# Merged prefix scans with resetting columns, turn counting on ScalarE and permuted reads in a two-expert kernel

## The chip, the cores and the metric

The kernel runs on one core of a Trainium2 chip. The metric is device time in microseconds (us) of one execution. The core has TensorE (PE in the profile, its weight loads PEld), VectorE (DVE), ScalarE (ACT), GpSimd (POOL) and SyncE (SP), which here only issues DMAs.

## The reference

A gated linear attention with a complex decay, followed by two dense expert layers:

```python
# attention: q, k, v, a_re, a_im are [4, 8, 768, 48] float32
mag = np.sqrt(a_re * a_re + a_im * a_im)
scale = np.minimum(mag, 0.999) / (mag + 1e-06)
a_re_n, a_im_n = (a_re * scale, a_im * scale)
for t in range(S):
    ar, ai = (a_re_n[:, :, t, :, None], a_im_n[:, :, t, :, None])
    new_re = ar * S_re - ai * S_im
    new_im = ar * S_im + ai * S_re
    kv = np.einsum('bhd,bhe->bhde', k[:, :, t], v[:, :, t])
    S_re, S_im = (new_re + kv, new_im)
    y[:, :, t] = np.einsum('bhd,bhde->bhe', q[:, :, t], S_re)
# x = y as [3072, 384]
x = (sigmoid(x @ w_gate) * (x @ w_val)) @ w_out      # first expert, d_ff 1536
h = x @ w_in
out = (h * sigmoid(h)) @ w2_out                      # second expert, d_ff 2048
```

The expert weights are float64 in memory; x is float32.

## The kernel before

**Attention in chunks.** The 3072 tokens are cut into 24 chunks of 128 time steps (`C = 128`), six for each batch element (`CPB = 6`); a chunk holds all 8 heads, so it has 384 columns (48 features times 8 heads). Each step's decay is taken apart into a magnitude m and a phase. Within a chunk the recurrence becomes matrix products, for which every key is scaled by the product of the magnitudes behind it (suffix product r), every query by the product up to it over the whole chunk's product (p), and both are turned by the summed phase f.

**Stages of a chunk.** Each is a function `s_...`, and a table of "beats" (`sched`, `starts`) says in which beat a chunk's stage is emitted, so that several chunks are under way at once. `s_nat1`, `s_nat2`, `s_nat2b` (L428 to L473) compute magnitude and tangent with time on the partitions; L472 writes the magnitudes m. `s_nat3` (L478) takes the arctangent on ACT. `s_perm` (L425) copies k and q on ACT. L472, L478 and L425 change the order of the columns from head-major to feature-major: they read in the order of memory and write with a stride of 8 elements (`perm`, L415). `s_den1` (L486 to L514) transposes m and the phases on PE into two PSUM tiles (`tr4`, L480: time now runs along the columns, 3 blocks of 128 partitions), and DVE scans each of the 3 blocks: three reversed scans for r (L500), three for p (L506), three for f (L510), each over 127 or 128 columns. Between them it multiplies out the chunk's whole product `pe` (L502, L503) and inverts it (L504). The phase sum is brought into one turn by three DVE instructions over 384 columns (L511 to L513: scale and add a large constant, subtract it and scale, subtract from f), and its last column is kept for the next chunk (`ca`, L514). `s_den2` takes sines on ACT (L520 to L522). `s_den3` (L524) transposes k and q, multiplies, copies the chunk's product behind the scaled keys (L533, L534), and 12 DMAs on SP regroup the result by head (`kst`, `qst`, L546). `s_mix1` to `s_mix3` are the products on PE (`ps_k` L559, `ps_a` L565, `ps_s`, `ps_y`), masked on DVE (L566).

**PSUM.** The attention's PSUM tiles (`ps_t`, `ps_k`, `ps_a`, `ps_s`, `ps_y`) share one pool of 3 buffers (`patt`, L374). The two tiles that `s_den1` scans are two of these three until the scans have read them.

**Experts.** A float64 weight tile is loaded by SP, turned into a float32 with rounding by ACT, DVE and POOL (`w_decode`, L338 to L341), and split into two parts (`w_split`, L347 on ACT, L348 on DVE or POOL in turn). Every product is three matmuls of such parts (`mm3`, L363 to L365). The first expert runs over nine blocks of 2 or 3 chunks, 12 steps of f each; in a step the gate's product `ps_g`, its tanh (L820, ACT), the value's product `ps_v`, their product `sg` (L823, DVE, which frees `ps_v`), the two parts `hh` (L829, ACT) and `hl` (L831, DVE), and the product back into `acc`. Between the halves of the steps the beats of later chunks are emitted. The second expert (L853 to L907) begins when attention is over; its weight tiles take the SBUF that attention leaves.

**Order.** PE's instructions run in the order in which the program emits them. The order on DVE, ACT, POOL and SP is set by a planner, which lists instructions by a simulated time line. Each engine then works through its list in order: an instruction that waits holds up all behind it.

Of the kernel before, what the change touches and what calls it, by code (L numbers as in the profile page):

```python
# [9 lines left out]
F32 = mybir.dt.float32  # L10
F32R = mybir.dt.float32r
I32 = mybir.dt.int32
U32 = mybir.dt.uint32
AF = mybir.ActivationFunctionType
ALU = mybir.AluOpType
# [230 lines left out]
def tile_kernel(ctx, tc, q, k, v, a_re, a_im, w_gate, w_val, w_out, w2_in, w2_out, out):  # L246
# [6 lines left out]
    F2 = w2_in.shape[1] // 256  # L253
    KD = DM // 128
    C = 128
    NCH = NT // C
    CPB = S // C
    R2 = 2 * D
# [116 lines left out]

    vz = stk.tile([128, H, EA], F32, tag="vz", name="vz")
    sdz = stk.tile([R2, H, EA], F32, tag="sdz", name="sdz")
    for t in (vz, sdz):
        G.memset(t, 0.0)
    ch = [dict() for _ in range(NCH)]  # L380
    RAMP = CFG["ramp"]

# [30 lines left out]
            ch[c][nm] = x  # L413

    def perm(t):  # L415
        return t.rearrange("p (d h) -> p h d", h=H)

    def heads(t):
        return t.rearrange("p (h d) -> p h d", h=H)

    def s_perm(c):
        z = ch[c]
        for nm in ("k", "q"):
            t = new(c, nat, [128, DM], nm + "p")
            A.copy(perm(t), z[nm])  # L425
            z[nm + "p"] = t

    def s_nat1(c):  # L428
# [48 lines left out]
        need(ATAN if c >= RAMP else TRIG)  # L477
        lut(A.activation(perm(z["X"][:, 0]), heads(z["Y"][:, 0]), AF.Arctan, scale=-1.0))  # L478

    def tr4(src):  # L480
        ps = patt.tile([128, KD, C], F32, tag="att", name="ps_t")
        for j in range(KD):
            PE.transpose(ps[:, j, :], src[:, j * 128:(j + 1) * 128], ident)
        return ps

    def s_den1(c):  # L486
        z = ch[c]
        mT = tr4(z["m"])
        pT = tr4(z["X"][:, 0])
        p_ = new(c, den, [128, KD, C], "p")  # L490
        rx = new(c, den, [128, KD, C + 1], "r")
        r_ = rx[:, :, 0:C]
        f_ = new(c, den, [128, KD, C], "f")
        n_ = new(c, den, [128, KD, C], "n")
        pe_ = den.tile([128, 2, KD], F32, tag="pe", name="pe", bufs=2)
        ca_ = den.tile([128, KD], F32, tag="ca", name="ca", bufs=2)
        z.update(p=p_, rx=rx, f=f_, n=n_, pe=pe_, ca=ca_)
        V.memset(r_[:, :, C - 1:C], 1.0)
        for j in range(KD):
            V.tensor_tensor_scan(  # L500
                r_[:, j, 0:C - 1][:, ::-1], mT[:, j, 1:C][:, ::-1], mask[:, 0:C - 1], 1.0, ALU.mult, ALU.bypass)
        V.tensor_tensor(pe_[:, 0], r_[:, :, 0], mT[:, :, 0], ALU.mult)  # L502
        V.tensor_scalar(pe_[:, 0], pe_[:, 0], TINY, None, ALU.max)  # L503
        V.reciprocal(pe_[:, 1], pe_[:, 0])  # L504
        for j in range(KD):
            V.tensor_tensor_scan(  # L506
                p_[:, j, :], mT[:, j, :], mask, pe_[:, 1, j:j + 1], ALU.mult, ALU.bypass)
        for j in range(KD):
            init = 0.0 if c % CPB == 0 else ch[c - 1]["ca"][:, j:j + 1]
            V.tensor_tensor_scan(f_[:, j, :], pT[:, j, :], mask, init, ALU.add, ALU.bypass)  # L510
        V.tensor_scalar(n_, f_, INV_2PI, MAGIC, ALU.mult, ALU.add)  # L511
        V.tensor_scalar(n_, n_, MAGIC, TWO_PI, ALU.subtract, ALU.mult)
        V.tensor_tensor(f_, f_, n_, ALU.subtract)  # L513
        V.tensor_copy(ca_, f_[:, :, C - 1])  # L514

    def s_den2(c):
        z = ch[c]
        n_, f_ = z["n"], z["f"]
        need(SIN if c >= RAMP else TRIG)
        lut(A.activation(n_, f_, AF.Sin, scale=UNIT))  # L520
        lut(A.activation(f_, f_, AF.Sin, scale=UNIT / 2))
        A.activation(f_, f_, AF.Square, scale=math.sqrt(2.0))  # L522

    def s_den3(c):  # L524
        z = ch[c]
        n_, f_, p_, rx = z["n"], z["f"], z["p"], z["rx"]
        r_ = rx[:, :, 0:C]
        kT = tr4(z["kp"])
        qT = tr4(z["qp"])
        kc = new(c, den, [128, KD, C + 1], "kc")  # L530
        V.tensor_tensor(r_, r_, kT, ALU.mult)
        V.tensor_tensor(p_, p_, qT, ALU.mult)
        V.tensor_copy(kc[:, :, C], z["pe"][:, 0])  # L533
        V.tensor_copy(rx[:, :, C], z["pe"][:, 0])  # L534
        V.scalar_tensor_tensor(kc[:, :, 0:C], f_, 1.0, r_, ALU.subtract, ALU.mult)
        G.tensor_tensor(r_, n_, r_, ALU.mult)
        V.scalar_tensor_tensor(f_, f_, 1.0, p_, ALU.subtract, ALU.mult)
        G.tensor_tensor(n_, n_, p_, ALU.mult)
        if c < RAMP and c % 2:
            kst = xp.tile([128, H, C + 1], F32, tag="xl", name="kst")[:R2]  # L540
        else:
            kst = stk.tile([R2, H, C + 1], F32, tag="kst", name="kst")
        qst = stk.tile([R2, H, C], F32, tag="qst", name="qst", bufs=2)
        for t, dst, off in ((kc, kst, 0), (rx, kst, D), (f_, qst, 0), (n_, qst, D)):
            for j in range(KD):
                SP.dma_start(dst[off + j * DI:off + (j + 1) * DI], t[:, j, :])  # L546
        z.update(kst=kst, qst=qst)

    def s_mix1(c):
        z = ch[c]  # L550
        kst, qst = z["kst"], z["qst"]
        kn = new(c, stk, [128, H, R2], "kn")
        am = stk.tile([128, H, C], F32, tag="am", name="am")
        hh = H // 2

        def turn(g):
            ps = patt.tile([128, hh, R2], F32, tag="att", name="ps_k")
            for h in range(hh):
                PE.transpose(ps[:, h, :], kst[:, g * hh + h, 0:C], ident[:R2, :R2])  # L559
            A.copy(kn[:, g * hh:(g + 1) * hh], ps)  # L560

        def score(g):
            ps = patt.tile([128, hh, C], F32, tag="att", name="ps_a")
            for h in range(hh):
                PE.matmul(ps[:, h, :], kst[:, g * hh + h, 0:C], qst[:, g * hh + h, :], start=True, stop=True)  # L565
# [52 lines left out]
    def s_mix2a(c):  # L618
        z = ch[c]
        A.copy(spread(vz), tails(z["v"]))  # L620
        if c % CPB:
            sd = st2.tile([R2, H, D], F32, tag="sd", name="sd", bufs=1)
            V.tensor_tensor(
                sd, ch[c - 1]["st"], z["kst"][:, :, C:C + 1].to_broadcast([R2, H, D]), ALU.mult)
            z["sd"] = sd
            V.tensor_copy(spread(sdz), tails(sd))

# [48 lines left out]
    def beats_for(i):  # L676
        return pos(bstart[i] + blocks[i] - 1, "mix3") + 1

# [1 line left out]
    w1 = {}  # L680
    raws, decs = {}, {}
    order1 = [(f, j) for f in range(F1) for j in range(3)]
# [73 lines left out]
    with tc.manual_schedule(engines={getattr(mybir.EngineType, e) for e in CFG["man"]}):  # L756
# [92 lines left out]
        moe_out(*prev)  # L849
        finish1(*fin)  # L850

# [102 lines left out]
```

## Time and profile before

| | us |
|---|---|
| median of 3 runs | 1206.17 (1203.48 to 1208.49) |
| span of the profiled execution | 1202.7 |
| PE busy in it | 1073.7 (89%) |
| DVE busy | 795.2 (66%) |
| ACT busy | 636.0 (53%) |
| POOL busy | 265.3 (22%) |

The span runs from the first to the last instruction of one execution; a run's time has what lies around it too. Shares of the whole span mix stages with different limits, so the rows below are by stage. Busy times of one engine can overlap by some tens of ns from one instruction to the next: a mean duration is longer than busy time over count.

### The profile page before, as it was taken

Reading aid. Unit: us, or ns where it says so; the run is one execution under the profiler, and the core shown is the slowest. Engines: PE = TensorE matmul, PEld = TensorE weight load, DVE = VectorE, ACT = ScalarE, POOL = GpSimd, SP = SyncE. Lnnn points to the kernel's source line nnn. Section 1 sums busy time; section 2 is a strip of 40 time slices with the busy share of each in tenths; the row PEclk is TensorE's granted clock in tenths of the full one; section 3 lists DMA queues with packets and bytes.
Section 4 is the critical chain, followed back from the end, with each engine's and each line's share of the span. In section 5 each row is a group of like instructions: output and inputs, shape, how many; then the busy total and the mean of one; then the engine's idle time right before and its main releaser. Section 6 shows DMA issues by size and latency. Waiting matters only on the chain. (4 is left out here: it accounts for less than half of the span.)

```text
span 1202.7 us, 21016 instructions
## 1 busy us (share of the span) xinstructions
PE 1073.7 (89%) x7814; PEld 1043.9 (87%) x7814; DVE 795.2 (66%) x1625; ACT 636.0 (53%) x1213; POOL 265.3 (22%) x258
## 2 busy tenths in 40 slices
PE   0376689999999999999999987899999999999997
PEld 0266579998999999999999987789999999999997
DVE  7899988688767866768667389977643434434343
ACT  5566677556666555566564255577533333333332
POOL 6555643222222222222221056500000000000000
PEclk9988799999999999999999999999999999999999
DMA  9256533343322333433221236599310101000000
GB/s 239 80 148 167 137 85 76 63 108 80 74 60 61 94 71 68 95 71 80 61 47 54 67 135 214 174 368 372 136 33 8 40 2 40 25 15 20 1 21 23
DMA packets 216765, 111.63 MB, mean 93 GB/s; under 512 B 132304, under 2 KB 209488, under 8 KB 216656
## 3 DMA queue, kind: packets, MB, share of 16 engines
q1 hardware_dynamic: 216656, 110.21, 33.8%
q8 instruction: 64, 1.05, 0.4%
q14 instruction: 45, 0.37, 0.1%
HBM read 81.79 MB, written 9.44 MB: 76 GB/s over the span
## 5 line engine op out<-in xcount | busy, mean ns | idle before, releaser
L887 DVE SCALAR_TENSOR_TENSOR sg<-sg,ps_h 128x384 f32<-128x384 f32 x128 | 70.8, 553 | 143.0 <-ACT sg L885 142.9
L885 ACT ACTIVATE sg<-ps_h 128x384 f32<-128x384 f32 x128 | 63.0, 492 | 167.7 <-PE ps_h L365 167.7
L365 PE MATMUL acc<-w,hl 128*128 128x384 f32 x384 | 129.2, 336 | 0.4
L363 PE MATMUL acc<-w,hh 128*128 128x384 f32 x384 | 128.6, 335 | 0.6 <-ACT hh L891 0.6
L363 PE MATMUL ps_v<-xh,w 128*128 128x384 f32 (+1 forms) x324 | 112.0, 346 | 19.2 <-DVE sg L823 19.1
L364 PE MATMUL acc<-w,hh 128*128 128x384 f32 x384 | 128.3, 334 | 0.0
L363 PE MATMUL ps_h<-xh,w 128*128 128x384 f32 x384 | 128.3, 334 | 0.0
L365 PE MATMUL ps_h<-xh,w 128*128 128x384 f32 x384 | 128.3, 334 | 0.0
L364 PE MATMUL ps_h<-xl,w 128*128 128x384 f32 x384 | 128.3, 334 | 0.0
L364 PE MATMUL acc<-hl,w 128*128 128x384 f32 (+1 forms) x324 | 106.7, 329 | 14.6 <-DVE hl L831 14.6
L893 DVE TENSOR_TENSOR hl<-sg,hh 128x384 fp32r<-128x384 f32 x128 | 71.3, 557 | 63.0 <-ACT hh L891 62.9
L363 PE MATMUL ps_g<-xh,w 128*128 128x384 f32 (+1 forms) x324 | 109.2, 337 | 3.7 <-ACT sg L820 3.1
L829 ACT CAST hh<-sg 128x384 fp32r<-128x384 f32 (+1 forms) x108 | 51.2, 474 | 108.7 <-DVE sg L823 108.6
L364 PE MATMUL ps_g<-xl,w 128*128 128x384 f32 (+1 forms) x324 | 105.4, 325 | 3.1 <-DVE xl L645 3.1
L364 PE MATMUL ps_v<-xl,w 128*128 128x384 f32 (+1 forms) x324 | 106.2, 328 | 0.0
L365 PE MATMUL ps_v<-xh,w 128*128 128x384 f32 (+1 forms) x324 | 106.2, 328 | 0.0
L363 PE MATMUL acc<-hh,w 128*128 128x384 f32 (+1 forms) x324 | 104.9, 324 | 0.6 <-ACT hh L829 0.6
L365 PE MATMUL ps_g<-xh,w 128*128 128x384 f32 (+1 forms) x324 | 105.2, 325 | 0.0
L365 PE MATMUL acc<-hh,w 128*128 128x384 f32 (+1 forms) x324 | 104.5, 323 | 0.0
L823 DVE SCALAR_TENSOR_TENSOR sg<-sg,ps_v 128x384 f32<-128x384 f32 (+1 forms) x108 | 54.4, 504 | 69.0 <-PE ps_v L365 69.0
L891 ACT CAST hh<-sg 128x384 fp32r<-128x384 f32 x128 | 65.6, 513 | 61.9 <-DVE sg L887 61.1
L341 POOL TENSOR_TENSOR raw<-raw,rnd 128x384 int32<-128x384 int32 x68 | 78.5, 1157 | 85.3 <-ACT rnd L338 33.2
(134 smaller groups left out, 2937.3 us busy)
## 6 DMA issues: line engine op xcount, KB each, us to landing
raw<-in_moe_w_out_dram SPq DMA_DIRECT2D x56, 384.0 KB, 6.6
raw<-in_moe_w_in_dram SPq DMA_DIRECT2D x32, 384.0 KB, 8.0
raw<-in_moe_w_gate_dram SPq DMA_DIRECT2D x24, 384.0 KB, 6.0
raw<-in_moe_w_val_dram SPq DMA_DIRECT2D x24, 384.0 KB, 6.4
kst<-kc SPq DMA_DIRECT2D x72, 64.5 KB, 2.7
kst<-r SPq DMA_DIRECT2D x72, 64.5 KB, 2.9
ri<-in_a_re_dram SPq DMA_DIRECT2D x24, 192.0 KB, 3.8
ri<-in_a_im_dram SPq DMA_DIRECT2D x24, 192.0 KB, 3.9
```

What stands on the lines that cost most here:

```text
L341: G.tensor_tensor(hi, hi, rnd, ALU.add)
L363: PE.matmul(o, lhi, rhi, start=first, stop=False)
L364: PE.matmul(o, lhi, rlo, start=False, stop=False)
L365: PE.matmul(o, llo, rhi, start=False, stop=last)
L823: V.scalar_tensor_tensor(sg[:, :n], sg[:, :n], 1.0, psv[:, :n], ALU.add, ALU.mult)
L829: A.copy(hh[:, :n], sg[:, :n])
L885: lut(A.activation(sg[:, :BT2], ps[:, :BT2], AF.Tanh, scale=0.5))
L887: V.scalar_tensor_tensor(sg[:, :BT2], sg[:, :BT2], 1.0, ps[:, :BT2], ALU.add, ALU.mult)
L891: A.copy(hh[:, :BT2], sg[:, :BT2])
L893: V.tensor_tensor(hl[:, :BT2], sg[:, :BT2], hh[:, :BT2].bitcast(F32), ALU.subtract)
```

## The change

- **Scans.** The transposed tiles get a 129th column in each of the 3 blocks (`CX = C + 1`), and one scan runs over all 387 columns (386 for p and f). In the extra column the magnitude is 0, so the running product is reset, and an added tensor restarts it: `edge` (1 in these columns) for r, `starts_` (the inverse of the chunk's product) for p. For f the multiplier `inner` is 0 there, and the phase tile holds the carried phase. So r now includes its own step, its first column is the chunk's product, and what reads r is shifted by a column. `edge`, `inner` and `starts_` are filled once, on POOL.
- **Around the scans.** DVE fills the extra columns of both PSUM tiles (a memset, and a copy or memset) and inverts 3 columns; L498, L502, L503 and the two copies L533, L534 go. One copy of the chunk's product into `kc` is made by ACT.
- **Turns.** ACT multiplies f by 1/(2 pi) and writes an int32; DVE subtracts that many turns in one instruction.
- **Permutation.** L472, L478 and L425 write contiguously and read with a stride of 48 elements (L472 from two inputs).

```diff
     def perm(t):
-        return t.rearrange("p (d h) -> p h d", h=H)
+        return t.rearrange("p (d h) -> p d h", h=H)
     def heads(t):
-        return t.rearrange("p (h d) -> p h d", h=H)
+        return t.rearrange("p (h d) -> p d h", h=H)
...
-            A.copy(perm(t), z[nm])
+            A.copy(perm(t), z[nm].rearrange("p h d -> p d h"))
...
-        V.memset(r_[:, :, C - 1:C], 1.0)
-        for j in range(KD):
-            V.tensor_tensor_scan(
-                r_[:, j, 0:C - 1][:, ::-1], mT[:, j, 1:C][:, ::-1], mask[:, 0:C - 1], 1.0, ALU.mult, ALU.bypass)
-        V.tensor_tensor(pe_[:, 0], r_[:, :, 0], mT[:, :, 0], ALU.mult)
-        V.tensor_scalar(pe_[:, 0], pe_[:, 0], TINY, None, ALU.max)
-        V.reciprocal(pe_[:, 1], pe_[:, 0])
-        for j in range(KD):
-            V.tensor_tensor_scan(
-                p_[:, j, :], mT[:, j, :], mask, pe_[:, 1, j:j + 1], ALU.mult, ALU.bypass)
-        for j in range(KD):
-            init = 0.0 if c % CPB == 0 else ch[c - 1]["ca"][:, j:j + 1]
-            V.tensor_tensor_scan(f_[:, j, :], pT[:, j, :], mask, init, ALU.add, ALU.bypass)
-        V.tensor_scalar(n_, f_, INV_2PI, MAGIC, ALU.mult, ALU.add)
-        V.tensor_scalar(n_, n_, MAGIC, TWO_PI, ALU.subtract, ALU.mult)
-        V.tensor_tensor(f_, f_, n_, ALU.subtract)
+        V.memset(mT[:, :, C:CX], 0.0)
+        if first:
+            V.memset(pT[:, 0:KD - 1, C:CX], 0.0)
+        else:
+            V.tensor_copy(pT[:, 0:KD - 1, C], ch[c - 1]["ca"][:, 1:KD])
+        V.tensor_tensor_scan(flat(rx)[:, ::-1], flat(mT)[:, ::-1], edge[:, ::-1], 0.0, ALU.mult, ALU.add)
+        V.reciprocal(starts_[:, 0:KD * CX:CX], rx[:, :, 0])
+        N = KD * CX - 1
+        V.tensor_tensor_scan(flat(p_)[:, :N], flat(mT)[:, :N], starts_[:, 1:], starts_[:, 0:1], ALU.mult, ALU.add)
+        V.tensor_tensor_scan(
+            flat(f_)[:, :N], inner[:, :N], flat(pT)[:, :N], 0.0 if first else ch[c - 1]["ca"][:, 0:1], ALU.mult, ALU.add)
+        f_ = f_[:, :, 0:C]
+        A.activation(n_.bitcast(I32), f_, AF.Copy, scale=INV_2PI)
+        V.scalar_tensor_tensor(f_, n_.bitcast(I32), -TWO_PI, f_, ALU.mult, ALU.add)
         V.tensor_copy(ca_, f_[:, :, C - 1])
...
-        V.tensor_copy(kc[:, :, C], z["pe"][:, 0])
-        V.tensor_copy(rx[:, :, C], z["pe"][:, 0])
-        V.scalar_tensor_tensor(kc[:, :, 0:C], f_, 1.0, r_, ALU.subtract, ALU.mult)
+        A.copy(kc[:, :, 0], rx[:, :, 0])
+        V.scalar_tensor_tensor(kc[:, :, 1:CX], f_, 1.0, r_, ALU.subtract, ALU.mult)
```

## Rows read from the trace of the kernel before

**Rows 1.** Stretches: length, busy PE, PEld, DVE, ACT, POOL; PE clock; DMA
```profile
28.00:172.00 144.00, 88.95 (x718) 81.23 (x719) 134.22 (x266) 89.47 (x167) 82.64 (x75) 0.88 0.50 129
...
60.00:180.00 120.00, 84.53 (x730) 78.91 (x730) 111.77 (x221) 78.26 (x147) 68.05 (x60) 0.86 0.51 135
180.00:360.00 180.00, 168.98 (x1615) 164.39 (x1613) 135.18 (x322) 113.28 (x197) 42.41 (x42) 0.97 0.36 77
360.00:690.00 330.00, 319.89 (x2670) 311.10 (x2669) 225.34 (x518) 184.25 (x303) 67.60 (x67) 1.00 0.30 69
690.00:800.00 110.00, 92.97 (x490) 87.70 (x489) 97.77 (x146) 63.52 (x148) 53.62 (x48) 0.95 0.62 207
```

**Rows 2.** PE's waits, 60 to 180 us: total, times, longest
```profile
PE ps_v L363 <- DVE sg L823: 11.2, 3, 5.8
...
PE acc L364 <- DVE hl L831: 5.0, 2, 2.6
```

**Rows 3.** DVE by line and shape, 28 to 172 us: busy, mean ns, idle before
```profile
L500 DVE TENSOR_TENSOR_SCAN r<-ps_t,mask 128x127 f32<-128x127 f32 x18 | 6.3, 400 | 2.4 <-PE ps_t L483 2.4
L506 DVE TENSOR_TENSOR_SCAN p<-ps_t,pe,mask 128x128 f32<-128x128 f32 x15 | 6.1, 457 | 0.0
L510 DVE TENSOR_TENSOR_SCAN f<-ps_t,ca,mask 128x128 f32<-128x128 f32 x14 | 5.7, 454 | 0.0
...
L472 DVE SCALAR_TENSOR_TENSOR T<-X,Y 128x384 f32<-128x384 f32 x6 | 5.1, 858 | 0.0
...
L511 DVE TENSOR_SCALAR n<-f 128x384 f32<-128x384 f32 x5 | 4.0, 798 | 0.0
...
L535 DVE SCALAR_TENSOR_TENSOR kc<-f,r 128x384 f32<-128x384 f32 x5 | 3.6, 710 | 2.9 <-ACT f L522 2.9
L513 DVE TENSOR_TENSOR f<-f,n 128x384 f32<-128x384 f32 x5 | 3.5, 709 | 0.0
...
L512 DVE TENSOR_SCALAR n<-n 128x384 f32<-128x384 f32 x5 | 2.9, 581 | 0.0
...
L533 DVE COPY kc<-pe 128x3 f32<-128x3 f32 x5 | 2.3, 450 | 0.0
...
L503 DVE TENSOR_SCALAR pe<-pe 128x3 f32<-128x3 f32 x5 | 1.6, 321 | 0.0
L534 DVE COPY r<-pe 128x3 f32<-128x3 f32 x5 | 1.2, 230 | 0.0
```

**Rows 4.** DVE by line and shape, whole span, one operation at two widths
```profile
L823 DVE SCALAR_TENSOR_TENSOR sg<-sg,ps_v 128x384 f32<-128x384 f32 x72 | 39.6, 550 | 51.3 <-PE ps_v L365 51.3
...
L823 DVE SCALAR_TENSOR_TENSOR sg<-sg,ps_v 128x256 f32<-128x256 f32 x36 | 14.8, 412 | 17.7 <-PE ps_v L365 17.7
```

**Rows 5.** PE's waits, 180 to 690 us
```profile
PE ps_a L565 <- DVE p L506: 11.6, 13, 0.9
PE ps_k L559 <- DVE p L506: 7.7, 5, 1.6
...
PE ps_v L363 <- DVE sg L823: 0.8, 2, 0.5
```

**Rows 6.** DVE in order of time: start, length, instruction; one chunk's r and p
```profile
374.81 1.05 DVE L500 TENSOR_TENSOR_SCAN r<-ps_t,mask 128x127 f32<-128x127 f32 x3 [1.57 <-PE ps_t L483]
...
379.13 1.22 DVE L506 TENSOR_TENSOR_SCAN p<-ps_t,pe,mask 128x128 f32<-128x128 f32 x3
```

**Rows 7.** PE in order of time, idle before in brackets: two waits
```profile
229.06 0.55 PE L559 MATMUL ps_k<-ident,kst 96*128 96x96 f32 x4 [1.58 <-DVE p L506]
...
380.40 1.16 PE L565 MATMUL ps_a<-qst,kst 96*128 96x128 f32 x8 [0.92 <-DVE p L506]
```

**Rows 8.** Stretches behind the first of these waits
```profile
228.00:231.00 3.00, 1.94 (x14) 1.94 (x15) 2.25 (x6) 1.74 (x4) 0.00 (x0) 0.87 0.00 0
231.00:234.00 3.00, 3.00 (x17) 3.00 (x17) 0.43 (x2) 2.97 (x6) 0.00 (x0) 0.56 0.00 0
```

**Rows 9.** ACT by line and shape, whole span
```profile
L425 ACT COPY kp<-k 128x384 f32<-128x384 f32 x24 | 22.0, 915 | 0.6 <-PE ps_t L483 0.4
...
L520 ACT ACTIVATE n<-f 128x384 f32<-128x384 f32 x24 | 12.5, 523 | 30.0 <-DVE f L513 30.0
```

**Rows 10.** ACT's waits, 180 to 690 us
```profile
ACT n L520 <- DVE f L513: 18.2, 18, 1.6
```

More of the change, by code (lines that the diff above doesn't have):

```diff
@@ L12 @@
 I32 = mybir.dt.int32
+U8 = mybir.dt.uint8
 U32 = mybir.dt.uint32
@@ L255, in tile_kernel @@
     C = 128
+    CX = C + 1
     NCH = NT // C
@@ L377, in tile_kernel @@
     sdz = stk.tile([R2, H, EA], F32, tag="sdz", name="sdz")
-    for t in (vz, sdz):
+    edge = stk.tile([128, KD * CX], U8, tag="edge", name="edge")
+    inner = stk.tile([128, KD * CX], U8, tag="inner", name="inner")
+    starts_ = stk.tile([128, KD * CX], F32, tag="starts", name="starts")
+    for t in (vz, sdz, edge, starts_):
         G.memset(t, 0.0)
+    G.memset(inner, 1)
+    G.memset(edge.rearrange("p (k c) -> p k c", c=CX)[:, :, C], 1)
+    G.memset(inner.rearrange("p (k c) -> p k c", c=CX)[:, :, C], 0)
     ch = [dict() for _ in range(NCH)]
@@ L478, in s_nat3, with tr4, flat @@
         lut(A.activation(perm(z["X"][:, 0]), heads(z["Y"][:, 0]), AF.Arctan, scale=-1.0))
-    def tr4(src):
-        ps = patt.tile([128, KD, C], F32, tag="att", name="ps_t")
+    def tr4(src, cols=C):
+        ps = patt.tile([128, KD, cols], F32, tag="att", name="ps_t")
         for j in range(KD):
-            PE.transpose(ps[:, j, :], src[:, j * 128:(j + 1) * 128], ident)
+            PE.transpose(ps[:, j, 0:C], src[:, j * 128:(j + 1) * 128], ident)
         return ps
+    def flat(t):
+        return t.rearrange("p k c -> p (k c)")
@@ L486, in s_den1 @@
     def s_den1(c):
         z = ch[c]
[L488 to L493, printed above, removed]
+        first = c % CPB == 0
+        mT = tr4(z["m"], CX)
+        pT = tr4(z["X"][:, 0], CX)
+        p_ = new(c, den, [128, KD, CX], "p")
+        rx = new(c, den, [128, KD, CX], "r")
+        f_ = new(c, den, [128, KD, CX], "f")
         n_ = new(c, den, [128, KD, C], "n")
-        pe_ = den.tile([128, 2, KD], F32, tag="pe", name="pe", bufs=2)
@@ L505, in s_den1 @@
[L505 to L513 removed]
+        z.update(p=p_, rx=rx, f=f_, n=n_, ca=ca_)
@@ L517, in s_den2 @@
         z = ch[c]
-        n_, f_ = z["n"], z["f"]
+        n_, f_ = z["n"], z["f"][:, :, 0:C]
         need(SIN if c >= RAMP else TRIG)
@@ L525, in s_den3 @@
         z = ch[c]
-        n_, f_, p_, rx = z["n"], z["f"], z["p"], z["rx"]
-        r_ = rx[:, :, 0:C]
+        n_, f_, p_, rx = z["n"], z["f"][:, :, 0:C], z["p"][:, :, 0:C], z["rx"]
+        r_ = rx[:, :, 1:CX]
         kT = tr4(z["kp"])
         qT = tr4(z["qp"])
-        kc = new(c, den, [128, KD, C + 1], "kc")
+        kc = new(c, den, [128, KD, CX], "kc")
         V.tensor_tensor(r_, r_, kT, ALU.mult)
         V.tensor_tensor(p_, p_, qT, ALU.mult)
-        V.tensor_copy(kc[:, :, C], z["pe"][:, 0])
-        V.tensor_copy(rx[:, :, C], z["pe"][:, 0])
-        V.scalar_tensor_tensor(kc[:, :, 0:C], f_, 1.0, r_, ALU.subtract, ALU.mult)
+        A.copy(kc[:, :, 0], rx[:, :, 0])
+        V.scalar_tensor_tensor(kc[:, :, 1:CX], f_, 1.0, r_, ALU.subtract, ALU.mult)
         G.tensor_tensor(r_, n_, r_, ALU.mult)
@@ L539, in s_den3 @@
         if c < RAMP and c % 2:
-            kst = xp.tile([128, H, C + 1], F32, tag="xl", name="kst")[:R2]
+            kst = xp.tile([128, H, CX], F32, tag="xl", name="kst")[:R2]
         else:
-            kst = stk.tile([R2, H, C + 1], F32, tag="kst", name="kst")
+            kst = stk.tile([R2, H, CX], F32, tag="kst", name="kst")
         qst = stk.tile([R2, H, C], F32, tag="qst", name="qst", bufs=2)
@@ L558, in turn @@
             for h in range(hh):
-                PE.transpose(ps[:, h, :], kst[:, g * hh + h, 0:C], ident[:R2, :R2])
+                PE.transpose(ps[:, h, :], kst[:, g * hh + h, 1:CX], ident[:R2, :R2])
             A.copy(kn[:, g * hh:(g + 1) * hh], ps)
@@ L564, in score @@
             for h in range(hh):
-                PE.matmul(ps[:, h, :], kst[:, g * hh + h, 0:C], qst[:, g * hh + h, :], start=True, stop=True)
+                PE.matmul(ps[:, h, :], kst[:, g * hh + h, 1:CX], qst[:, g * hh + h, :], start=True, stop=True)
             V.tensor_tensor(
@@ L623, in s_mix2a @@
             V.tensor_tensor(
-                sd, ch[c - 1]["st"], z["kst"][:, :, C:C + 1].to_broadcast([R2, H, D]), ALU.mult)
+                sd, ch[c - 1]["st"], z["kst"][:, :, 0:1].to_broadcast([R2, H, D]), ALU.mult)
             z["sd"] = sd
```

1 line of the change is left out of this document (removed).

## The prediction

> **What bounds the kernel now.** I read the stretches first, because the shares of the whole span mix four stages [rows 1]. From 28 to 172 us DVE is busy for 134.2 of 144 us while PE is busy for 89.0: the ramp is bound by DVE, which decodes the first expert's weights and does the vector work of the first chunks at once. What PE waits for longest there is DVE's list, not data: 11.2 us for `sg` and 5.0 us for `hl`, short instructions that stand behind others [rows 2]. PE also pays a second time, by its clock: 0.86 of full in 60 to 180 us. From 180 to 690 us PE is the bound: idle 11.0 of 180 and 10.1 of 330 us [rows 1]. Nearly all of this idle time has one cause: PE's next attention product waits for the p scan, 11.6 us in 13 places and 7.7 us in 5, 19.3 us in 18 chunks [rows 5]. The reader is to see why: `s_den1` holds two of the pool's three PSUM buffers until its scans are through, and p, on which the wait ends, comes last. In the chunk at 374.81 us the r scans begin then, the p scans begin at 379.13 and end 1.22 us later, 5.5 us in all; PE starts at 380.40, having waited 0.92 us [rows 6, 7]. From 690 to 800 us DVE is busy for 97.8 of 110 us, but with the second expert's weights, and that stage begins when PE's list reaches it; the change touches nothing in it or behind it. So two places can pay: the ramp, and the 18 waits.
>
> **The scans, priced.** No row has a scan longer than 128 columns, so its time must be bounded. L823 takes 412 ns for 256 columns and 550 ns for 384 [rows 4]: 1.08 ns a column, and 136 ns that don't depend on the length. From above: three scans of a kind take 1.05 us (r) or 1.22 us (p) end to end [rows 6], and a merged one can't cost more than that. From below: a scan of 127 columns takes 400 ns [rows 3], and at 1.08 ns for each further column 387 would take 0.68 us. Between: if the scan has the same 136 ns of its own as L823, it spends 264 ns on 127 columns, 2.08 ns each, and 387 columns take 0.94 us. I take this, since the fixed part is the only thing that merging removes and a row gives its size; p with its pointer start takes 57 ns more [rows 3], and so does f. Busy time counts the 80 ns or so by which neighbours overlap only once, so I book 0.9 us for each, 2.7 us a chunk. [...]
>
> **What DVE saves in the ramp.** Five chunks have all of `s_den1` between 28 and 172 us (L506 is there 15 times, and a sixth chunk's r scans: L500 is there 18 times) [rows 3]. Removed or replaced, by busy time: r 5.3 (15/18 of 6.3), p 6.1, f 5.7 for 14 scans, so 6.1 for 15; L511, L512, L513 10.4; L503 1.6; L533 and L534 3.5. Together 33.0 us, 6.6 a chunk. That these cost far more than their size (L533 takes 450 ns for 3 columns) is time lost beside POOL, and it goes with them. The other tiny ones (L498 and L502 go, a memset and a copy on PSUM come) I set against each other; the inversion and `ca` stay. Added: three scans 2.7 us, and the one instruction that subtracts the turns, like L535 in this stretch 0.71 us: 3.4 a chunk, 17.0. DVE saves 33.0 - 17.0 = 16 us of 134.
>
> How much of it reaches the end? DVE is idle for only 9.8 us of the stretch [rows 1], so its list shortens by nearly that amount, and PE has 55 us of idle time there to give. But the planner draws up a new list, and the ramp also needs loads, ACT and POOL in turn. I take 12 us; the bounds are 3 (most of it comes back as DVE idle time) and 20 (PE's clock, 0.88 in this stretch, recovers with it).
>
> **What the 18 waits give.** In the new order p needs the memset, one r scan, the inversion and its own scan: 0.9 + 0.2 + 0.9 us, and 0.9 more if f is put between, as it is now. With half a us of other work that makes some 3.4 us from the r scan's start to the buffer's release, where it was 5.5. That is 2.1 us earlier, and the longest of the waits is 1.6 us [rows 5]. So I count all 19.3 us but about one, 18; next late is then `sg`, which costs PE 0.8 us in this whole stretch [rows 5]. If the planner put p behind other work, half of it stays: 9.
>
> **The clock behind the waits.** [...] Over 180 to 360 us the clock is 0.97, a loss of 5.4 us; from 360 us on, where the waits are 0.9 us, it is 1.00 [rows 1]. I count 4 us, from 0 to 5.4.
>
> **Parts at nothing.** ACT gains the turn count, about L520's 523 ns [rows 9], and a tiny copy; it is busy 89 of 144 us in the ramp and 297 of 510 us behind it [rows 1], so the cover is its idle time. Without it 24 x 0.7 = 17 us would show. The permuted reads: L425 takes 915 ns against L520's 523 for as many columns [rows 9], so the permuted write costs ACT 0.4 us in each of three instructions; whether a permuted read costs less, no row shows. For ACT the ends are 1.2 us saved and nothing, off the path either way. For DVE L472 takes 858 ns [rows 3] against 550 for L823's like [rows 4]: at best 0.3 us a chunk saved, at worst, with two inputs that pay as the output did, 0.3 lost: 1.5 us each way in the ramp; I take zero. [...] The few fills at the start of POOL's list I take at nothing too.
>
> **The sum.** 1202.7 - 12 - 18 - 4 = 1168.7 us of span. The median of the runs lies 3.5 us above the profiled span, which gives 1172.
>
> **Rivals.**
> - Only the waits go: the ramp gives DVE's time back as waits for POOL, ACT or loads. 1206 - 18 - 4 + 1 for a reordered ramp: 1185. For it: POOL is busy 82.6 of 144 us there; against it: DVE is busy for 93% [rows 1].
> - Only the ramp pays: p is put behind f, the turns and an expert's instruction, as now, and the release moves by too little. 1206 - 12 = 1194. Against it: at 2.1 us earlier there is 0.5 us to spare even for the longest wait.
> - Neither pays, because the merged scan costs as much as three and the planner's new list eats the rest: 1206 - 3 = 1203, no change that can be told.
> - Slower: the turn count is a round trip, DVE to ACT and back, in two lists that run in order. ACT now waits 1.0 us a chunk for f (18.2 us in 18) [rows 10]; in the new order DVE's subtraction waits for ACT in turn, and behind it stand `sg`, which frees `ps_v`, and `hl`. It costs nothing as long as other DVE work is put between. If ACT is held by a tanh, a cast or a table load, DVE stands for up to 2 us a chunk; in the ramp that is 10 us against 12, and in the steady stage it becomes 18 new waits of the size of the old or larger. Slower begins where PE loses more than 34/24 = 1.4 us a chunk; at 2 us it is 1172 + 48 = 1220. Against it: ACT is idle 42% of the steady stage [rows 1].
>
> **How the numbers follow.** Both places pay 0.54, only the waits 0.18, only the ramp 0.08, neither 0.09, slower 0.11. Predicted 1172. The low end takes the upper bounds of all terms, 1206 - 20 - 19.3 - 5.4, and a little of the cheaper scan: 1158. The high end takes in both half cases: 1199. Outside lie neither and slower, 0.20. A measurement of this kernel can tell 0.5%, 6 us, from no change: faster 0.80, same 0.09, slower 0.11.
>
> **What would show each step.** A scan of 387 columns near 0.94 us; DVE busy in the ramp some 16 us less, and the last decode of the first expert some 12 us earlier; no PE wait on p behind the ramp; clock 1.00 from 180 to 360 us. I would be wrong if DVE showed idle time ahead of the subtraction of the turns, or PE a new wait on `sg` or on a PSUM fill.

## The result and the profile after

The changed kernel takes 1171.8 us (median of 4 runs, 1169.68 to 1172.73), the kernel before 1206.07 us beside it: a ratio of 0.9715, 95% interval 0.9693 to 0.9738. The profiled span went from 1202.7 to 1171.0 us, by 31.7 us.

The stretches of the kernel after, in the same columns and at the same moments as [rows 1] (length, busy PE, PEld, DVE, ACT, POOL with instruction counts, granted PE clock, DMA share, GB/s):

```profile
28.00:172.00 144.00, 96.20 (x779) 88.23 (x780) 130.08 (x220) 99.05 (x188) 89.76 (x74) 0.87 0.51 132
...
180.00:360.00 180.00, 177.79 (x1693) 174.09 (x1693) 132.79 (x263) 123.92 (x224) 42.34 (x43) 1.00 0.39 84
360.00:690.00 330.00, 324.73 (x2637) 318.47 (x2637) 222.65 (x409) 191.38 (x333) 78.30 (x77) 0.99 0.32 79
```

From 180 to 360 us PE was idle for 11.0 us before and is idle for 2.2 us now, at a granted clock of 1.00 in place of 0.97. The rows for 28 to 172 and 360 to 690 us can't be compared so simply: work has moved forward into them (PE has 779 instructions in the first in place of 718), and the last one now reaches into the next stage.

PE's waits from 180 to 690 us after (engine, line, releaser: total, times, longest), for comparison with [rows 5]:

```profile
PE ps_v L365 <- DVE sg L830: 4.2, 4, 3.0
PE acc L366 <- DVE hl L838: 3.1, 4, 1.4
```

The 18 waits on p, 19.3 us, are gone. (Of the 4.2 us on `sg`, 3.4 lie behind 645 us, in the next stage; `sg` had 0.8 before [rows 5].) One chunk after shows why, first on DVE and then on PE (start, length, instruction), beside [rows 6, 7]:

```profile
430.51 0.96 DVE L513 TENSOR_TENSOR_SCAN r<-ps_t,edge 128x387 f32<-128x387 f32 x1
...
431.68 1.02 DVE L517 TENSOR_TENSOR_SCAN f<-inner,ca,ps_t 128x386 f32<-128x386 uint8 x1
432.62 1.00 DVE L516 TENSOR_TENSOR_SCAN p<-ps_t,starts 128x386 f32<-128x386 f32 x1
```

```profile
433.63 0.49 PE L566 MATMUL ps_k<-ident,kst 96*128 96x96 f32 x4
433.96 1.98 PE L572 MATMUL ps_a<-qst,kst 96*128 96x128 f32 x16
```

From the start of the r scan to the end of the last scan 3.1 us pass; it was 5.5 us, and in that chunk PE had waited 0.92 us. The products of this one start at 433.63 with no idle time ahead.

To see where the 31.7 us come from, the two executions must be cut at the same work, not at the same time. I use three marks: the last decode of the first expert's weights (`raw`, L340 before, L342 after) and the first DVE instruction that writes an expert block's output (`xo`, L713 before, L720 after), for blocks 1, 3, 7 and the first block of the second expert. Between the same marks of before (columns as above):

```profile
28.00:156.82 128.82, 78.57 (x651) 71.81 (x651) 121.16 (x243) 79.66 (x148) 71.30 (x65) 0.88 0.49 130
...
190.91:318.17 127.26, 118.70 (x1169) 115.84 (x1170) 96.14 (x233) 80.83 (x142) 29.65 (x30) 0.96 0.37 80
318.17:644.83 326.66, 314.99 (x2593) 306.09 (x2592) 234.04 (x544) 196.06 (x317) 72.47 (x72) 1.00 0.32 72
...
644.83:844.31 199.48, 181.89 (x1133) 175.57 (x1132) 150.09 (x258) 111.89 (x279) 55.84 (x50) 0.97 0.62 208
```

and of after:

```profile
28.00:150.45 122.45, 78.92 (x658) 71.80 (x659) 111.44 (x189) 84.72 (x161) 78.96 (x65) 0.87 0.53 140
...
183.00:298.52 115.52, 113.31 (x1166) 110.67 (x1166) 88.52 (x180) 82.12 (x149) 29.63 (x30) 1.00 0.40 86
298.52:610.58 312.06, 310.19 (x2590) 304.45 (x2589) 216.85 (x413) 200.99 (x340) 71.03 (x72) 1.00 0.34 75
...
610.58:813.23 202.65, 183.18 (x1133) 176.69 (x1132) 150.66 (x251) 113.45 (x283) 55.65 (x50) 0.97 0.61 207
```

PE's instruction counts agree to 3 in 2593 from block 1 on, so these are the same pieces of work. They give the account:

| piece | before | after | difference |
|---|---|---|---|
| up to the end of block 1 | 190.91 | 183.00 | -7.9 |
| block 1 to block 3 | 127.3 | 115.5 | -11.7 |
| block 3 to block 7 | 326.7 | 312.1 | -14.6 |
| block 7 to the second expert's first block | 199.5 | 202.7 | +3.2 |

From there the difference stays at -31.1 us (the last block: 1195.07 and 1163.92). Below, "the ramp" is the first piece, "the steady part" the two from block 1 to block 7, together -26.3 us, and "the switch" the last.

### The profile page after: what moved, and what is told of

It is laid out like the page before. It is cut to its first block, busy times and chain, and to the rows that moved or that the text cites. A ratio compares the mean times of both kernels' runs of the same rounds, so it can differ in the third digit from the quotient of the medians.

```text
span 1171.0 us, 20843 instructions
## 1 busy us (share of the span) xinstructions
PE 1065.2 (91%) x7814; PEld 1039.0 (89%) x7814; DVE 758.5 (65%) x1361; ACT 648.8 (55%) x1261; POOL 270.6 (23%) x263
## 3 DMA queue, kind: packets, MB, share of 16 engines
q8 instruction: 64, 1.05, 0.4%
## 5 line engine op out<-in xcount | busy, mean ns | idle before, releaser
L365 PE MATMUL ps_v<-xh,w 128*128 128x384 f32 (+1 forms) x324 | 110.7, 342 | 14.6 <-DVE sg L830 14.3
L365 PE MATMUL ps_g<-xh,w 128*128 128x384 f32 (+1 forms) x324 | 107.9, 333 | 8.1 <-ACT sg L827 7.5
L367 PE MATMUL ps_v<-xh,w 128*128 128x384 f32 (+1 forms) x324 | 104.8, 324 | 0.0
L343 POOL TENSOR_TENSOR raw<-raw,rnd 128x384 int32<-128x384 int32 x68 | 84.3, 1241 | 86.3 <-ACT rnd L340 33.2
L367 PE MATMUL ps_g<-xh,w 128*128 128x384 f32 (+1 forms) x324 | 103.4, 319 | 0.0
```

The source lines that it names most:

```text
L343: G.tensor_tensor(hi, hi, rnd, ALU.add)
L365: PE.matmul(o, lhi, rhi, start=first, stop=False)
```

## The experiments

The question is which part of the change pays, and by which way. Two theories stood against each other for the steady part: the release of the PSUM buffers (theory R: PE's 18 waits go because p ends sooner behind the chunk's first scan) and the load (theory L: DVE simply has less to do, so all that PE needs from it comes sooner). For the ramp the question is why 7.9 us came and not the 12 that were forecast. Every ratio that follows is to the kernel before, run beside it. Each of these kernels has its own list from the planner, so a difference of a few microseconds between two of them need not come from the edit itself.

**One part of the change at a time.**

scans_only: after, but with the three DVE instructions for the turns and with permuted writes.

```diff
-A.activation(n_.bitcast(I32), f_, AF.Copy, scale=INV_2PI)
-V.scalar_tensor_tensor(f_, n_.bitcast(I32), -TWO_PI, f_, ALU.mult, ALU.add)
+V.tensor_scalar(n_, f_, INV_2PI, MAGIC, ALU.mult, ALU.add)
+V.tensor_scalar(n_, n_, MAGIC, TWO_PI, ALU.subtract, ALU.mult)
+V.tensor_tensor(f_, f_, n_, ALU.subtract)
...
-            A.copy(perm(t), z[nm].rearrange("p h d -> p d h"))
+            A.copy(perm(t), z[nm])
```

> The changed kernel with the three turn instructions back on DVE and the permuted writes back; the merged scans and what belongs to them stay. Theory R: the release is still earlier than before, because seven instructions between r and p are gone, though the turn instructions may stand between: no waits on p behind the ramp or under 5 us in sum, 1173 to 1180 us. Theory L: the ramp has back some 1.4 us a chunk of DVE work and so does every later chunk: 1180 to 1190 us.

Measured: 1181.56 us, 0.9810 [0.9787, 0.9833]. The time lies just above the release theory's range, in the load theory's, as the ramp gives 2.3 of the 7.9 us; but PE has no wait on p left from 185 to 645 us, as the release theory wants. Ramp -2.3 us, steady part -22.5.

turns_only: before, with the turns counted on ACT (the same five lines, the other way round).

> The kernel before with only the turn count moved: ACT makes the int32, DVE subtracts in one instruction; nine scans and permuted writes stay. Theory R: of the three turn instructions that stood between r and p (some 1.6 us with what they wait for) at least two go, the release comes 1 us or more earlier, and waits of 0.9 us go, those of 1.6 us shrink: 1180 to 1190 us. Theory L: DVE saves 10.4 - 3.5 = 7 us in the ramp, two thirds of which shows: 1199 to 1203 us.

Measured: 1183.02 us, 0.9829 [0.9806, 0.9853], as the release theory had it. Ramp -5.2 us, steady part -17.8. Here nine scans are still in place, yet PE's waits on p from 185 to 645 us have shrunk to 1.1 us in 4 places and 1.0 in one. The buffer with the magnitudes is held for 4.7 us per chunk (median, from the start of the r scan to the end of the last reader) where it was 5.55: with waits of 1.07 us on average (19.3/18), 0.85 us earlier takes most of each away. That is the point at which the two parts overlap. By the ratios scans_only saves 0.0190 x 1205 = 22.9 us and turns_only 20.6, together 43.5, but the whole change 0.0285 x 1206 = 34.4. The overlap is in the steady part (22.5 + 17.8 against 26.3); in the ramp the two add up (2.3 + 5.2 against 7.9). Either part alone removes most of the same 18 waits, and the second finds them gone.

perm_only: before, with permuted reads. after_writes: after, with permuted writes. no_order: after, with contiguous reads and writes, and so without the change of column order.

```diff
     def perm(t):
-        return t.rearrange("p (d h) -> p h d", h=H)
+        return t.rearrange("p (d h) -> p d h", h=H)
     def heads(t):
-        return t.rearrange("p (h d) -> p h d", h=H)
+        return t.rearrange("p (h d) -> p d h", h=H)
...
-            A.copy(perm(t), z[nm])
+            A.copy(perm(t), z[nm].rearrange("p h d -> p d h"))
```

> The kernel before with only the permutation turned from writes into reads. Both theories: the copies of k and q on ACT stay near 0.9 us and L472 near 0.88 us, as in the changed kernel, and the time stays within 1202 to 1210 us. If permuted reads were what pays (a third theory, P), 1190 us or less.

> The changed kernel with the permutation back in the writes; scans and turn count stay as changed. If the direction of the permutation is worth nothing, as its own run beside the kernel before says, 1170 to 1174 us, L433 at 0.91 to 0.94 instead of 0.88 us. If it pays once ACT has the turn count too: 1176 us or more.

```diff
-        return t.rearrange("p (d h) -> p d h", h=H)
+        return t.rearrange("p (d h) -> p (d h)", h=H)
...
-        return t.rearrange("p (h d) -> p d h", h=H)
+        return t.rearrange("p (h d) -> p (h d)", h=H)
...
-            A.copy(perm(t), z[nm].rearrange("p h d -> p d h"))
+            A.copy(perm(t), z[nm].rearrange("p h d -> p (h d)"))
```

> The changed kernel with the change of column order left out altogether: L480, L486 and the copies of k and q read and write contiguously, so the columns keep the head-major order and the output is another one. It gives the price of the order change itself: the copies on ACT should take 0.52 us instead of 0.88 (0.36 us saved, three times a chunk) and L480 0.55 instead of 0.88 us. The time: the ramp gains 5 x 0.3 us on DVE, 1168 to 1173 us; 1160 or less would say that ACT's length matters after all.

Measured: perm_only 1206.35 us, 1.0007 [0.9983, 1.003]; after_writes 1175.47 us, 0.9734 [0.9693, 0.9775]; no_order 1170.77 us, 0.9713 [0.9685, 0.9742]. The copy on ACT and the product on DVE by line and shape (busy, mean ns, idle before), in perm_only:

```profile
L425 ACT COPY kp<-k 128x384 f32<-128x384 f32 x24 | 21.0, 876 | 0.7 <-PE ps_t L483 0.5
```

```profile
L472 DVE SCALAR_TENSOR_TENSOR T<-X,Y 128x384 f32<-128x384 f32 x24 | 21.1, 881 | 1.4 <-POOL Y L468 1.2
```

and in no_order:

```profile
L433 ACT COPY kp<-k 128x384 f32<-128x384 f32 x24 | 12.2, 507 | 0.1
```

```profile
L480 DVE SCALAR_TENSOR_TENSOR T<-X,Y 128x384 f32<-128x384 f32 x24 | 13.2, 551 | 1.5 <-POOL Y L476 1.3
```

A permuted read costs what the permuted write cost: 876 against 915 ns on ACT [rows 9], 881 against 894 on DVE (whole span, before). Against contiguous access both cost 0.3 to 0.4 us more, and even that whole price, taken off three instructions a chunk on ACT and one on DVE, moves the time by an amount that can't be told from nothing (0.9713 against 0.9715). after_writes came out between its two forecasts, at 1175.47 us, and its interval includes the ratio of after. So this part of the change is neutral as far as these runs can tell, and its cover is what the prediction took it to be.

**Order without load.** p_first: before, with nothing removed; only the f scans are made to stand behind the p scans in DVE's list.

```diff
-            V.tensor_tensor_scan(
+            last_p = V.tensor_tensor_scan(
                 p_[:, j, :], mT[:, j, :], mask, pe_[:, 1, j:j + 1], ALU.mult, ALU.bypass)
...
-            V.tensor_tensor_scan(f_[:, j, :], pT[:, j, :], mask, init, ALU.add, ALU.bypass)
+            fs = V.tensor_tensor_scan(f_[:, j, :], pT[:, j, :], mask, init, ALU.add, ALU.bypass)
+            tc.add_manual_dep(unwrap(fs), unwrap(last_p).name, NOSYNC, reason="p ahead of f")
```

> The kernel before with one order forced: each chunk's three f scans are listed behind its three p scans. All nine scans, the three turn instructions and the permuted writes stay, so DVE's work is the same. Theory R (release): what PE loses behind the ramp is the time until the p scan lets go of a PSUM buffer; p is through about 1.2 us earlier and f later, so most of the 18.7 us of waits on p between 190 and 645 us go, and with them the low-clock stretches: 1184 to 1190 us. Theory L (load): the gain of the change comes from DVE having less to do; here it has the same, so 1203 to 1209 us, with the waits only renamed.

Measured: 1196.13 us, 0.9928 [0.9909, 0.9948], between the two forecasts. Its steady part, from block 1 to block 7 (columns as above), and PE's longest waits from 185 to 645 us; both are given in this part for every kernel:

```profile
198.28:634.32 436.04, 426.60 (x3753) 415.58 (x3752) 329.00 (x778) 274.73 (x456) 101.03 (x102) 1.00 0.35 76
```

```profile
PE acc L364 <- DVE hl L832: 3.9, 7, 1.0
PE ps_a L566 <- DVE p L506: 3.2, 5, 1.0
```

The kernel before has DVE busy for 330.2 us over the same work and PE idle for 20.2; here DVE is busy for 329.0 and PE idle for 9.4. The buffer with the magnitudes is held for 2.9 us, the one with the phases, whose scans now come last, for 4.05. So 17.9 us of the steady part's 26.3 come with no DVE work removed at all: the order of two scans was most of the loss. The ramp, on the other hand, got 7.4 us longer with the same work, because the planner's list came out differently there, and that takes nearly half of the gain away again. The load theory can't explain the first number.

**Load with and without the release.** Both kernels are after with two more scans a chunk, 386 columns each, written to a tile that is overwritten later. In late_release they read the magnitudes in PSUM (`mT`, the edit shown), and so hold the buffer; in same_load they read r in SBUF (`rx` in its place).

```diff
+        z["kc"] = kc = new(c, den, [128, KD, CX], "kc")
+        for _ in range(2):
+            V.tensor_tensor_scan(flat(kc)[:, :N], flat(mT)[:, :N], starts_[:, 1:], starts_[:, 0:1], ALU.mult, ALU.add)
...
-        kc = new(c, den, [128, KD, CX], "kc")
+        kc = z["kc"]
```

> The changed kernel with two more scans of 386 columns a chunk that read the PSUM tile of the magnitudes and write a tile that is overwritten later. DVE has 24 x 1.9 us more to do, and the PSUM buffer is let go up to 1.9 us later. Theory R: PE's waits for that buffer come back behind the ramp, 0.3 to 1.5 us in each of 18 chunks, 8 us or more in sum, and with the longer ones the clock falls below 1.00 between 180 and 360 us; with some 6 us for the load in the ramp 1184 to 1200 us. Theory L: the same time as same_load, within 3 us.

> The changed kernel with the same two extra scans a chunk, but reading r in SBUF instead of the PSUM tile: the same load for DVE, no longer hold on the PSUM buffer. Theory R: no waits for the buffer behind the ramp unless the planner puts the extra scans ahead of p; the load costs 5 x 1.9 us in the ramp, of which some two thirds show: 1175 to 1182 us, at least 8 us under late_release. Theory L: as late_release, within 3 us.

Measured: late_release 1212.74 us, 1.0068 [1.0047, 1.009]; same_load 1197.39 us, 0.9947 [0.993, 0.9965]. Both are slower than the release theory allowed (at most 1200 and 1182), and they are 15.3 us apart, where the load theory had at most 3. For late_release the steady part, and PE's waits:

```profile
186.86:644.30 457.44, 432.30 (x3762) 420.49 (x3761) 334.90 (x623) 289.40 (x492) 100.62 (x102) 0.99 0.34 73
```

```profile
PE ps_a L575 <- DVE ca L525: 14.3, 10, 1.7
PE ps_k L569 <- DVE ca L525: 6.9, 5, 1.5
```

for same_load:

```profile
194.92:638.99 444.07, 428.44 (x3759) 416.53 (x3760) 334.86 (x624) 287.80 (x493) 101.40 (x102) 1.00 0.35 75
```

```profile
PE ps_k L569 <- ACT kn L570: 7.8, 12, 0.8
PE ps_v L365 <- DVE sg L833: 5.4, 4, 1.7
```

In late_release the old waits are back in number and size: 15 of them, up to 1.7 us, 21.2 us in all, before the same PE products (`ca` is the instruction right behind the second extra scan and is through with it), and two more, 1.7 us, are put down to that scan. The buffer is held for 5.86 us, a little longer than in the kernel before. With the same instructions and the buffer held for 3.1 us, same_load has none of these waits; in the steady part the two differ by 13.4 us (+3.5 against -9.9, both to the kernel before), which is the price of the release at an equal load: DVE is busy for 334.9 us in both. (The whole times differ by more; the ramp and the switch, where the list came out differently, have their share in that.) But same_load isn't back at 1175 to 1182 us, where the release theory put it: it is 26 us above the kernel after. Its trace shows the load's own way to PE, first on DVE, then on ACT, then on PE (idle time before and its releaser in brackets):

```profile
428.44 1.14 DVE L519 TENSOR_TENSOR_SCAN kc<-r,starts 128x386 f32<-128x386 f32 x1
429.50 0.52 DVE L833 SCALAR_TENSOR_TENSOR sg<-sg,ps_v 128x384 f32<-128x384 f32 x1
```

```profile
430.06 0.51 ACT L839 CAST hh<-sg 128x384 fp32r<-128x384 f32 x1 [1.89 <-DVE sg L833]
...
430.95 0.46 ACT L570 COPY kn<-ps_k 128x384 f32<-128x384 f32 x1
```

```profile
431.47 0.55 PE L569 MATMUL ps_k<-ident,kst 96*128 96x96 f32 x4 [0.62 <-ACT kn L570]
```

`sg` stands behind the extra scan on DVE; ACT's list stands at `hh`, which needs `sg`; behind `hh` stands the copy that frees the third PSUM buffer; and PE waits for that one. The same three buffers, held up by another of their users.

load_away: to keep the extra work away from both, the two scans were moved into `s_den3`, behind the products with k and q, where no PSUM tile waits for them.

```diff
         V.tensor_tensor(p_, p_, qT, ALU.mult)
+        N = KD * CX - 1
+        for _ in range(2):
+            V.tensor_tensor_scan(
+                flat(kc)[:, :N], flat(z["p"])[:, :N], starts_[:, 1:], starts_[:, 0:1], ALU.mult, ALU.add)
```

> The changed kernel with two extra scans a chunk of the same length as in same_load, reading p in SBUF, but listed in the stage behind, after the products with k and q, where no PSUM buffer and no instruction of PE's next product waits for them. Theory R in its sharper form (PE loses behind the ramp only what stands on DVE between the transposes and the release of a PSUM buffer, sg and the mask included): from the end of the first block to that of the seventh it keeps nearly all the change's gain, 22 us or more against before, where same_load kept 10; the load shows in the ramp, 6 to 12 us: 1176 to 1185 us. Theory L (any DVE work costs, wherever it stands): as same_load, 1194 to 1200 us.

Measured: 1214.24 us, 1.0069 [1.0043, 1.0095], above what either theory allowed. The steady part, and PE's waits:

```profile
202.01:652.99 450.98, 432.96 (x3769) 420.07 (x3769) 334.94 (x626) 284.93 (x491) 111.81 (x102) 1.00 0.34 74
```

```profile
PE ps_v L365 <- DVE sg L834: 9.2, 8, 2.3
PE ps_k L570 <- ACT kn L571: 5.3, 9, 0.7
```

PE waits on the scans' own buffers only once, for 0.5 us, but `sg` is late by up to 2.3 us, and the ramp is 11.1 us longer than before. The steady part is 3.0 us shorter than before, where the release theory put 22 or more. The extra work was not away from everything, either: ACT's copy into `kc` stands behind the extra scans, and ACT waits for them 13 times, 6.5 us in all. So neither theory holds by itself. Side by side, over the same work from block 1 to block 7, sorted by DVE's busy time ("hold": from the start of the r scan to the end of the last reader of the magnitudes, median):

| kernel | DVE busy | hold | PE idle | what PE waits for most |
|---|---|---|---|---|
| after | 305.4 | 3.1 | 4.1 | hl |
| scans_only | 317.1 | 3.1 | 5.0 | sg, hl |
| turns_only | 321.6 | 4.7 | 6.9 | hl, sg, p |
| p_first | 329.0 | 2.9 | 9.4 | hl, p |
| before | 330.2 | 5.5 | 20.2 | p |
| same_load | 334.9 | 3.1 | 15.6 | kn, sg |
| late_release | 334.9 | 5.9 | 25.1 | the last reader of the magnitudes |
| load_away | 334.9 | 3.1 | 18.0 | sg, kn |

Both DVE's work and the hold count. At nearly the same DVE work PE is idle for 10.8 us less in p_first than in before, and for 9.5 us less in same_load than in late_release: that is the hold. At a hold of 3.1 us PE's idle time grows from 4.1 to 15.6 and 18.0 us with DVE's work: that is the load. It comes through short instructions that PE needs next, and how much stands ahead of them in DVE's list. The change helps in two ways: it puts p's scan 2.45 us closer to the first scan, and it leaves less that can stand ahead of `sg` (read from same_load and load_away, in which more stood there).

**The ramp.** ca_act: after, with the copy of the carried phase (3 columns) on ACT. This copy is one of the cheapest instructions of `s_den1` and was the one that had grown most in the ramp. In the kernel before, DVE by line, 28 us to the last decode:

```profile
L514 DVE COPY ca<-f 128x3 f32<-128x3 f32 x5 | 0.8, 154 | 0.0
```

and after, the lines of `s_den1` over the same piece of work:

```profile
L516 DVE TENSOR_TENSOR_SCAN p<-ps_t,starts 128x386 f32<-128x386 f32 x5 | 5.0, 1007 | 0.1
L513 DVE TENSOR_TENSOR_SCAN r<-ps_t,edge 128x387 f32<-128x387 f32 x5 | 4.8, 959 | 0.1
...
L517 DVE TENSOR_TENSOR_SCAN f<-inner,ca,ps_t 128x386 f32<-128x386 uint8 x4 | 4.0, 999 | 0.0
...
L521 DVE SCALAR_TENSOR_TENSOR f<-n,f 128x384 f32<-128x384 int32 x5 | 3.5, 696 | 0.0
...
L522 DVE COPY ca<-f 128x3 f32<-128x3 f32 x5 | 3.1, 628 | 0.0
```

```diff
-        V.tensor_copy(ca_, f_[:, :, C - 1])
+        A.copy(ca_, f_[:, :, C - 1])
```

> The changed kernel with the copy of the carried phase moved from DVE to ACT. In the ramp this copy of 3 columns is busy 3.1 us in 5 chunks, 0.63 us each, against 0.15 us where nothing is beside it. Theory M (time lost beside POOL moves to the next DVE instruction when one is taken away): DVE saves only its own 0.15 us a chunk, the time stays within 1170 to 1174 us, and what DVE's instructions lose in the ramp over their shortest lengths stays at 27 us or more. Theory G (it goes with the instruction): 3 us less in the ramp, 1167 to 1169 us.

Measured: 1169.45 us, 0.9692 [0.9654, 0.9729], between the two ranges; ramp -7.8 us against the kernel before, where after has -7.9. Taking the 3.1 us off DVE leaves the ramp as it was, so the copy was only where the lost time showed. The median is 2.3 us below after's, which these intervals can't tell from nothing.

Where the time is lost can be read from the trace. One of the three long copies in the ramp of the kernel after, and what POOL does meanwhile:

```profile
46.20 0.97 DVE L522 COPY ca<-f 128x3 f32<-128x3 f32 x1
```

```profile
45.82 1.33 POOL L350 TENSOR_TENSOR w<-raw,w 128x384 fp32r<-128x384 f32 x1
```

The copy begins while POOL is at work and ends 0.02 us after POOL has ended. I took all DVE instructions from 28 us to the last decode that last over 100 ns longer than the shortest of their line and shape. There are 54 before, 49 after and 52 in ca_act. All but one each in after and ca_act begin beside a POOL instruction, and end behind the end of one by no more than that shortest length. Together they lose 34.4 us before, 28.6 after and 31.7 in ca_act, 30.9 to 35.1 in the others. In ca_act (its last decode comes 2.5 us later, with two more instructions ahead of it) those outside `s_den1` lose 30.9 us where they lost 25.5 in after: the loss passed from the copy to others.

## Why the prediction was right, and where its steps were not

Forecast 1172 us, measured 1171.8. The two places were right, and so was the mechanism of the larger one. That the numbers agree so closely is luck, as four errors cancel: the ramp was booked 4.1 us too high, the steady part 4.3 too low, the switch gave back 3.2 that were not foreseen, and the way from the span to the median was put 2.7 too long.

- **The price of the merged scan: right.** 0.94 us was taken between 0.68 and 1.05 (for p 1.22); the three take 0.96, 1.01 and 1.00 us in the ramp. The slope from 127 columns at 400 ns [rows 3] to 387 at 959 is 559/260 = 2.15 ns a column, where 2.08 was worked out from L823's fixed 136 ns; that is twice L823's 1.08 ns [rows 4]. The rows give 14.7 us for 15 scans where 13.5 were booked: they hold the overlap with the neighbours, which the booking had left out.
- **The 18 waits: right, and the clock with them.** Forecast 18 + 4 = 22 us, and the steady part gave 26.3. PE's idle time there fell from 20.2 to 4.1 us, 16.1 (forecast 18). From block 1 to 3 PE's busy time fell by 118.70 - 113.31 = 5.4 us with a clock of 1.00 in place of 0.96, of which the clock accounts, by an estimate from these two numbers, for 127.26 x 0.04 = 5.1: nearly the upper bound of that term. No run shows the 4 us that stood in the sum; in its place the traces show a clock of 0.50 for 3.4 us behind three of the five waits of 1.4 to 1.6 us in the kernel before (from 230.2 [rows 8], 278.0 and 301.9 us on), and of 1.00 from 183 to 610 us in the kernel after. The rest, 4.8 us, is a term that I hadn't: between blocks 3 and 7 the clock is 1.00 in both kernels, and PE is busy for 314.99 and 310.19 us with the same work. 3.2 us of it is a single line, `ps_a`, which is what waited. PE by line and shape (busy, mean ns, idle before), blocks 3 to 7, before:

```profile
L565 PE MATMUL ps_a<-qst,kst 96*128 96x128 f32 x192 | 26.9, 283 | 11.0 <-DVE p L506 11.0
```

and after:

```profile
L572 PE MATMUL ps_a<-qst,kst 96*128 96x128 f32 x192 | 23.7, 277 | 0.0
```

  The same 192 products cover 3.2 us less of the time line when none of them starts from a standstill: 0.27 us for each of the 12 waits, on top of the idle time that the view of waits shows. The length of the wait made no difference to this. In turns_only the same 12 breaks are down to 0.01 to 0.09 us each, too short for the view of waits, and the cover is that of before:

```profile
L564 PE MATMUL ps_a<-qst,kst 96*128 96x128 f32 x192 | 26.9, 283 | 0.9
```

  It is 26.9 us in late_release too, where the 12 waits add up to 16.0 us. (Ends of matmuls are modelled in this profile, so how a wait's cost is split between idle and busy time depends on that model; the sum of the two does not.) The mis-sized step is that I took the waits' idle time for their whole cost.
- **The mechanism of the waits: right, though not the only one.** The release came from 5.55 to 3.10 us (forecast 3.4), and late_release, whose extra scans differ from same_load's in one operand, brings back the waits and takes 13.4 us of the steady part. In the chunk shown f did stand between r and p, which the rival "only the ramp pays" feared; it did no harm. But what is next late is not just `sg` with 0.8 us as [rows 5] has it: same_load and load_away show that `sg` and what hangs on it come up to 2.3 us late as soon as DVE has more ahead of them. The forecast rested on a lighter DVE there without saying so.
- **The ramp: mis-sized, 7.9 for 12 us.** DVE's work was to fall by 16 us; up to the last decode its busy time fell by 9.7 (121.16 to 111.44). That is the step that failed, and its parts can be named. By line, `s_den1` and the two removed copies fell from 35.2 to 23.1 us, by 12.1: 1.2 of the missing us are the scans, and 2.7 the short instructions that I had set against each other, above all `ca`, 0.8 to 3.1 us. The other 2.4 us are overlap: a line's busy time holds the tens of ns by which an instruction overlaps a neighbour of another line, DVE's total counts them once, and I subtracted the removed lines as they stood. Counted once, these lines take 30.5 us before and 20.9 after, and all other DVE instructions 90.7 and 90.5. The sentence that the time lost beside POOL "goes with" the removed instructions was right for most of them and wrong for `ca`: by the measure above these lines lost 7.1 us before and 3.1 after, 2.35 of it at `ca`, which hadn't lost any before. The others lost 27.3 and 25.5; single ones did grow, L542 (before L535) from 710 ns [rows 3] to 1047. DVE's idle time rose by 3.4 us (7.7 to 11.0), which leaves 6.4 us by which the last decode came earlier, where the prediction had some 12. That the planner's new list can give back a part was allowed for in the bounds, and p_first shows how much that is: 7.4 us in the other direction for two scans swapped.
- **The switch: forecast unchanged, 3.2 us longer.** PE is busy for 1.3 us more there and idle for 1.9 us more. Over the other kernels this piece varies from -0.9 (perm_only) to +6.3 us (late_release) against before without a pattern that I can name: turns_only has +2.1, scans_only +0.1, ca_act +0.2, after_writes +2.8. That a new list of the planner causes it is an argument, not shown; the cause stays open.
- **ACT's round trip: no cost, as forecast.** ACT waited 2.7 us for f in the whole span (L520, 523 ns each), no DVE wait for its result shows, and turns_only gains with it. So the condition of the rival "slower" never came about, and its price was not tested.
- **Permuted reads: nothing, as forecast,** by perm_only and after_writes. On ACT the read with a stride of 48 floats took 876 ns and the write with a stride of 8 took 915, 39 ns apart, and no_order gives the price of the strided read, 876 - 507 = 369 ns for 384 columns.

So the sum read 1202.7 - 12 - 18 - 4, and the trace has 1202.7 - 7.9 - 16.1 - 5.4 - 4.8 + 3.2 = 1171.7 against a span of 1171.0; the remaining 0.7 lies behind the last mark and in rounding. The forecast's 1168.7 of span was 2.3 us too low, and the 3.5 us added for the median stood at 0.8 this time.

## What to carry to other kernels

Where an engine waits for another's in-order list, look first at how long a shared buffer is held and what stands between its first and its last reader: here two scans swapped gave 18 of the 26 us that a rewrite gave in that stage, though any new list of the planner may cost several us elsewhere. Subtract removed work by what the engine's busy time counts once, not by rows that overlap their neighbours. Don't count on saving all the time that an instruction loses to contention when you remove the instruction: as long as the other engine's work stays, some other instruction can run into it, as in ca_act, where the loss outside `s_den1` rose from 25.5 to 30.9 us. Parts of a change that attack the same wait don't add; run each alone before you credit it.

## What the runs showed of the hardware

- A break in PE's stream of `ps_a` products cost more than its idle time: 0.27 us for each of 12 breaks at full clock, seen as a longer cover of the same 192 products (26.9 against 23.7 us), whether a break lasted 0.01 to 0.09 us (turns_only), 0.9 (before) or up to 1.7 (late_release). Between blocks 1 and 3, where the waits of up to 1.6 us lay, PE took 5.4 us more for the same work at a granted clock of 0.96.
- DVE instructions that run long in the ramp run beside POOL and end just behind it: in the twelve kernels 49 to 58 last over 100 ns longer than the shortest of their line and shape, 628 in all, and 625 of these begin beside a POOL instruction and end behind the end of one by at most their own shortest length. In after, `ca` with 3 columns took from 158 to 975 ns, the three long ones ending 0.02 to 0.03 us behind POOL. The loss was 28.6 to 35.1 us of DVE's 111 to 123 busy us in the twelve kernels.
- The copy of k on ACT (128x384) took 876 ns reading with a stride of 48 floats (perm_only), 915 writing with a stride of 8 (before) and 507 with both contiguous (no_order). The product on DVE of the same size took 881 ns with two strided inputs, 894 with a strided output and 551 with all contiguous, in the same three kernels.
